# One load of a four-layer kernel's input, issued from ScalarE's queue in place of SyncE's

## The chip, the cores and the metric

The kernel runs on one core of a Trainium2 chip. The core has five engines with an instruction queue each: TensorE (PE, matrix products), VectorE (DVE), ScalarE (ACT), GpSimd (POOL) and SyncE (SP), which here does nothing but issue DMAs and wait. Loads and stores are carried by 16 DMA engines. The metric is the device time of one execution in microseconds; less is better. The profile comes from one further execution that the hardware profiler recorded.

## What is computed

Two blocks, run twice in turn on x of 2048 tokens by 512 features, in bfloat16. Each block normalises its input and adds its result to it.

```python
x = A_x
x = x + _A_ref(_layernorm(x, axis=-1), A_wqkv, A_wo)   # linear attention, 32 heads of 16
x = x + _B_ref(_layernorm(x, axis=-1), B_w1, B_w2)     # 512 -> 1376, relu, -> 512
x = x + _A_ref(_layernorm(x, axis=-1), A_wqkv, A_wo)
x = x + _B_ref(_layernorm(x, axis=-1), B_w1, B_w2)
```

In the attention block q, k and v are projections of the normalised x by `A_wqkv`; phi (t + 1 for positive t, exp(t) otherwise) is applied to q and k; k and v are summed over all tokens into one small matrix for each head, by which q is multiplied.

## The kernel before

The 2048 tokens are 16 tiles of 128 tokens, in four chunks of four tiles. x lies in `xin` with one tile in each of 16 slots. All operations of the four layers are put into a graph by `build_kernel`: each operation has an engine, what it reads and writes, and a cost. A planner (`_list_schedule`) then lays out each engine's order from these costs, from a table of hand-set priorities (`HINTS`) and a few fixed sequences (`SEQS`), and `emit_engine` writes one instruction stream for each engine, with semaphore waits where an operation needs another engine's result. Every DMA is an operation of SyncE, made by the helper `dma`, with a semaphore of its own that reaches 16 when the data has landed.

The start of the first layer is what the change and the prediction's steps touch. SyncE issues, in this order:

- tile 0 of x (`ld_x0_0`, line 744, 128 KB)
- tiles 1 to 3 of x (`ld_x0_1`, line 744, 384 KB)
- the k and q columns of `A_wqkv`, in two halves of the contraction (`ld_wqk0` and `ld_wqk1`, line 750, 512 KB each)
- tiles 4 and 5 (`ld_x1_0`, line 744, 256 KB)
- tiles 6 and 7 (`ld_x1_2`), which wait until tiles 1 to 3 have landed
- chunks 3 and 2 (512 KB each), behind the landing of the second and of the first half of the weights

```python
ld_x(0, 0, 1, 100.0)
wq_v = A_wqkv.rearrange("(c p) n -> p c n", p=128)
ld_x(0, 1, lat=1500.0)
```

Nothing before these loads is waited for but the barrier at the program's start.

Meanwhile TensorE runs warm-up matmuls on a constant (line 775), ScalarE waits for GpSimd's constant `nhalf` (line 783), loads its table of functions (line 763) and runs one small operation, and GpSimd sets up constants.

Chunk 0 is handled tile by tile. VectorE takes a tile's statistics (lines 802 and 803) and subtracts the mean (line 1554); for tile 3, ScalarE sums the tile and its squares instead (lines 1564 and 1566). TensorE transposes the centred tile (line 883), ScalarE or VectorE copies it from the accumulator memory into `Tb` (lines 887 and 888), and TensorE multiplies it by the weights (line 928, the helper that emits nearly all matrix products). GpSimd computes the reciprocal standard deviations (lines 1548 and 1550), which ScalarE applies when it reads the products (lines 910 and 912). VectorE's order begins with the statistics of tile 0, then those of tile 2, then the centring of tiles 2 and 3, and the statistics of tile 1. The products of k come in two halves, so that the first half of the weights can be used before the second has landed. From chunk 1 on, VectorE normalises whole tiles (lines 809, 845) and a DMA transpose that SyncE issues (line 866) fills `Tb`; the first of these waits for all weight loads.

## Time and profile before

| what | value |
|---|---|
| median of 3 runs | 267.29 us (267.24 to 267.83) |
| profiled execution, its own time | 267.75 us |
| span of the profile, first to last instruction | 266.0 us, 5120 instructions |
| TensorE busy | 260.9 us (98%) |
| VectorE, ScalarE, GpSimd busy | 215.4, 192.0, 51.2 us (81%, 72%, 19%) |
| DMA | 23.22 MB in 48122 packets, mean 87 GB/s |

Times in the profile are microseconds from the span's start. In a row of the timeline stand the start, the length, the engine, the line, the operation, what it writes and reads, the count, and in brackets the idle time of the engine just before with what ended it. "SPq" is SyncE's queue at a DMA issue; the transfer itself shows only as a wait of those who need the data ("DMA xin<-in_A_x_dram"). In a row of the windows stand the stretch, its length, the busy time (and count) of PE, PE's weight loads, DVE, ACT and POOL, the granted clock of TensorE, the busy share of the DMA engines, which can exceed 1 where transfers overlap, and GB/s. In a row of the DMA issues the last number is the time from issue to landing. The ends of matrix products are modelled, so a busy TensorE isn't one at its peak.

### The profile page before, as it was taken

The page shows a single profiled execution, that of the slowest core. Times are in us where ns is not written, and L with a number is a line of the kernel's source. Part 1 is how long each engine was busy: PE and PEld are TensorE (multiplying, and loading weights), DVE is VectorE, ACT ScalarE, POOL GpSimd, SP SyncE. Part 2 cuts the span into 40 slices and gives each one's busy share as a digit, 9 for nine tenths or more (in the row PEclk, how much of TensorE's full clock was granted, in tenths as well). Part 3 has the DMA queues.
Part 4 walks back from the last instruction along what each step waited for, and adds up shares of the span by engine and source line. Part 5 has one row for each costly group of instructions (what it writes and reads, how often), then busy time and mean ns, then how long its engine had stood idle before and what let it go on. Part 6 is the DMA issues. An engine that isn't in the chain of part 4 may idle for free.

```text
span 266.0 us, 5120 instructions
## 1 busy us (share of the span) xinstructions
PE 260.9 (98%) x1890; PEld 171.2 (64%) x1890; DVE 215.4 (81%) x557; ACT 192.0 (72%) x420; POOL 51.2 (19%) x131
## 2 busy tenths in 40 slices
PE   7999999999999999999999999999999999999996
PEld 3344444644755888767776744474488888888874
DVE  4897986799889999879786848479999888697865
ACT  4798899998975756898718689578599974656300
POOL 6410010012860023400001340001734040000000
PEclk9999999999999999999999999999999999999999
DMA  6744489866249023150000313054460501602104
GB/s 213 252 88 81 139 159 366 229 156 100 44 87 160 0 21 58 25 99 1 2 0 0 66 27 68 4 140 111 107 120 2 99 2 38 140 2 70 52 1 160
DMA packets 48122, 23.22 MB, mean 87 GB/s; under 512 B 38784, under 2 KB 45920, under 8 KB 48096
## 3 DMA queue, kind: packets, MB, share of 16 engines
q1 hardware_dynamic: 48096, 22.88, 37.2%
q8 instruction: 15, 0.25, 0.4%
q14 instruction: 11, 0.09, 0.1%
HBM read 7.14 MB, written 2.10 MB: 35 GB/s over the span
## 4 chain that ended last, share of the span: by engine, by line
PE 91%; DMA 4%; DVE 3%; SPq 1%; issue 0%; DVEq 0%
PE ps L928 91%; DMA xin<-in_A_x_dram 3%; DMA Tb<-xn 1%; DVE bst L802 1%; DVE big L921 1%; DVE xn L845 0%; DVE wqkv L944 0%; SPq L750 0%; SPq L744 0%; DVE escr L914 0%; DVE xn L1610 0%; DVE mv L803 0%; DVE veps L809 0%; DVEq L1822 0%
## 5 line engine op out<-in xcount | busy, mean ns | idle before, releaser
L928 PE MATMUL ps<-Tb,w 128*128 128x256 f16 (+2 forms) x240 | 42.0, 301 | 0.0
L1327 ACT ACTIVATE big<-ps 128x512 bf16<-128x512 f32 x58 | 33.0, 597 | 10.3 <-PE ps L928 10.0
L960 ACT ACTIVATE sqscr<-xres 128x512 bf16<-128x512 f32 x48 | 29.9, 626 | 9.6 <-DVE xres L954 9.4
L928 PE MATMUL ps<-w,big 128*128 128x256 bf16 (+5 forms) x213 | 36.5, 293 | 0.0
L928 PE MATMUL ps<-wqkv,Tb 128*128 128x512 bf16 x144 | 34.5, 379 | 0.9 <-DMA wqkv<-in_A_wqkv_dram 0.6
L928 PE MATMUL ps<-big,xn 128*128 128x512 bf16 (+1 forms) x160 | 31.2, 336 | 0.2 <-DVE veps L809 0.2
L910 ACT ACTIVATE big<-ps 128x512 bf16<-128x512 f32 x48 | 28.7, 603 | 1.5 <-PE ps L928 1.4
L928 PEld LDWEIGHTS ps<-Tb,w 128*128 128x128 f16 (+1 forms) x240 | 23.2, 98 | 9.3
L928 PE MATMUL ps<-xn,xin 128*128 128x256 f16 x168 | 28.8, 272 | 0.0
L1274 DVE TENSOR_TENSOR ps<-ps,escr 128x256 f32<-128x256 f32 x56 | 22.8, 427 | 7.1 <-PE ps L928 6.6
L912 ACT ACTIVATE escr<-ps 128x512 bf16<-128x512 f32 x44 | 25.7, 604 | 3.4 <-PE ps L928 3.3
L928 PE MATMUL ps<-Tb,wqkv 128*128 128x512 bf16 x112 | 27.1, 379 | 0.0
L825 POOL TENSOR_SCALAR mean<-s 128x4 f32<-128x4 f32 (+1 forms) x13 | 3.7, 285 | 117.4 <-DVE xres L954 117.3
L928 PE MATMUL ps<-Mf,big 128*128 128x512 bf16 x112 | 25.0, 379 | 0.0
L928 PEld LDWEIGHTS ps<-wqkv,Tb 128*128 128x128 bf16 x144 | 13.7, 98 | 16.5 <-DMA wqkv<-in_A_wqkv_dram 1.1
L928 PEld LDWEIGHTS ps<-w,big 128*128 128x128 bf16 (+1 forms) x213 | 20.3, 98 | 5.2
L928 PEld LDWEIGHTS ps<-big,xn 128*128 128x128 bf16 x160 | 15.1, 98 | 12.1 <-POOL xn L979 0.7
L928 PE MATMUL ps<-xin,big 128*128 128x256 bf16 x150 | 20.8, 272 | 0.0
L914 DVE TENSOR_SCALAR escr<-escr 128x512 bf16<-128x512 bf16 x52 | 14.3, 286 | 6.7 <-ACT escr L912 6.5
L928 PEld LDWEIGHTS ps<-Mf,big 128*128 128x128 bf16 x112 | 10.7, 98 | 12.7 <-DVE big L1105 0.3
L921 DVE TENSOR_TENSOR big<-big,escr 128x512 bf16<-128x512 bf16 x46 | 18.4, 417 | 0.2
L928 PEld LDWEIGHTS ps<-Tb,wqkv 128*128 128x128 bf16 x112 | 10.8, 98 | 11.7 <-issue 0.4
(139 smaller groups left out, 499.4 us busy)
## 6 DMA issues: line engine op xcount, KB each, us to landing
big<-rdc SPq DMA_DIRECT2D x32, 128.0 KB, 2.7
wqkv<-in_A_wqkv_dram SPq DMA_DIRECT2D x3, 512.0 KB, 5.0
w<-in_B_w_dram SPq DMA_DIRECT2D x1, 1376.0 KB, 7.6
w<-in_B_w_dram SPq DMA_DIRECT2D x1, 1280.0 KB, 10.8
xin<-in_A_x_dram SPq DMA_DIRECT2D x2, 512.0 KB, 4.5
out_dram<-wqkv SPq DMA_DIRECT2D x2, 512.0 KB, 3.5
xin<-in_A_x_dram SPq DMA_DIRECT2D x2, 256.0 KB, 6.2
wo<-in_A_wo_dram SPq DMA_DIRECT2D x1, 512.0 KB, 7.6
```

Source lines behind the costliest of these rows:

```text
L802: g.add(DVE, lambda e: e.bn_stats(bst[:, i, :], xin[:, i, :]), [("xin", i)] + list(after), [("bst", i)], C_DVE_BNST, name="bnst%d" % i)
L825: g.add(POOL, lambda e: e.tensor_scalar(mean[:, sl], s1[:, sl], -INV_D, None, ALU.mult), [("s1", i) for i in tl], [("mean", i) for i in tl ...
L910: g.add(ACT, lambda e: e.activation(dst_ap, psv[:, b, :], ACTF.Identity, bias=1.0 + 1e-6, scale=sc), [("ps", b)] + rk, [dst_key], C_ACT_PS ...
L912: g.add(ACT, lambda e: e.activation(esc, psv[:, b, :], ACTF.Exp, scale=sc), [("ps", b)] + rk, [ekey], C_ACT_EXP + xd, name=name + "_exp")
L914: g.add(DVE, lambda e: e.tensor_scalar(esc, esc, 1.0, 1e-6, ALU.min, ALU.add), [ekey], [ekey], C_DVE_BF4X, name=name + "_em")
L921: g.add(DVE, lambda e: e.tensor_tensor(dst_ap, dst_ap, esc, ALU.max), [dst_key, ekey], [dst_key], 340.0, name=name + "_phi")
L928: last = e.matmul(o, l, r, start=st, stop=sp, skip_group_check=skip)
L960: g.add(ACT, lambda e: e.activation(sqscr[:, q, :], xres[:, i, :], ACTF.Square, accum_out=s2[:, i:i + 1]), [("xres", i)], [("sqscr", q), ( ...
L1274: g.add(DVE, lambda e: e.tensor_tensor(psv[:, bank, 256:512], psv[:, Y, 0:256], m5, ALU.add), [("ps", Y), ("escr", s)], [("ps", bank)], C_ ...
L1327: g.add_flex([(ACT, lambda e: e.activation(unit_ap(u), psv[:, b, :], ACTF.Relu), C_ACT_PSUM), (DVE, lambda e: e.tensor_scalar(unit_ap(u), ...
```

## The change

The load of tiles 1 to 3 (`ld_x0_1`) is taken out of SyncE's stream and emitted as the first instruction of ScalarE's, with the same semaphore. The planner still sees the operation where it was, on SyncE and at the same cost, so every engine's order stays as it was; SyncE simply emits nothing at that place. The load waits for nothing, before or after. Those who wait for tiles 1 to 3 wait for the same semaphore.

```diff
+        ACT_LOADS = ('ld_x0_1',)
+        act_loads = []
...
             def _emit(eng, emit=emit, sem=sem):
                 return emit(eng).then_inc(sem, 16)
+            if g.layer == 0 and name in ACT_LOADS:
+                act_loads.append((ACT_LOADS.index(name), _emit))
+                _emit = lambda eng: None
             op = g.add(SP, _emit, reads, writes, dur=issue, lat=xfer_ns, dma=True, name=name)
...
             @block.scalar
             def _(s):
+                for _, load in sorted(act_loads, key=lambda a: a[0]):
+                    load(s)
                 emit_engine(ACT, s)
```

## The prediction

> **What bounds the kernel now.** I read the chain that ended last first, by line and then in order of time.

> ```profile
> by line: PE ps L928 91.1%; DMA xin<-in_A_x_dram 2.6%; DMA Tb<-xn 1.4%; DVE bst L802 0.9%; DVE big L921 0.5%; DVE xn L845 0.5%; DVE wqkv L944 0.4%; SPq L750 0.3%; SPq L744 0.3%; DVE escr L914 0.3%; DVE xn L1610 0.2%; issue 0.2%; DVE mv L803
> 0.79 0.40 SPq L744
> ...
> 1.25 0.41 SPq L744
> ...
> 1.71 0.43 SPq L750
> ...
> 2.18 0.47 SPq L750
> ...
> 2.69 6.87 DMA xin<-in_A_x_dram
> ...
> 9.58 1.29 DVE bst L802 x2
> ...
> 16.75 3.86 DMA Tb<-xn
> 20.61 0.05 issue
> 20.65 242.27 PE ps L928 x1790
> ```

> From 20.65 us on TensorE is the chain for 242 us, so the change is worth there what it moves the start of that stretch. Ahead of it lie five DMA issues, one after the other on SyncE. The second (1.25) is the load that moves; the fifth (2.69) is the first half of x's second chunk (tiles 4 and 5), which lands 6.87 us later and starts the statistics on VectorE at 9.58. From there to 16.75 the chain is VectorE's, and then a DMA transpose. Next, each engine in order of time:

> ```profile
> 2.88 0.69 DVE L802 BATCH_NORM_STATS2 bst<-xin 128x6 f32<-128x512 bf16 x1 [2.88 <-DMA xin<-in_A_x_dram]
> 3.83 0.35 DVE L1554 TENSOR_SCALAR xn<-xin,mv 128x512 bf16<-128x512 bf16 x1
> 4.66 0.70 DVE L802 BATCH_NORM_STATS2 bst<-xin 128x6 f32<-128x512 bf16 x1 [0.47 <-DMA xin<-in_A_x_dram]
> 7.99 0.42 DVE L888 COPY Tb<-ps 128x512 bf16<-128x512 bf16 x1
> 9.58 1.29 DVE L802 BATCH_NORM_STATS2 bst<-xin 128x6 f32<-128x512 bf16 x2 [1.18 <-DMA xin<-in_A_x_dram]
> 0.83 3.78 PE L775 MATMUL ps<-const-bfloat16-1.0 128*128 128x512 bf16 x9 [0.83 <-PEq L1877]
> 6.01 0.40 PE L883 MATMUL ps<-ident,xn 128*128 128x128 bf16 x4 [0.63 <-DVE xn L1554]
> 6.58 1.13 PE L928 MATMUL ps<-wqkv,Tb 128*128 128x512 bf16 x4
> 7.77 0.59 PE L928 MATMUL ps<-wqkv,Tb 128*128 128x512 bf16 x2
> 8.96 5.79 PE L928 MATMUL ps<-wqkv,Tb 128*128 128x512 bf16 x26 [0.60 <-DMA wqkv<-in_A_wqkv_dram]
> 14.95 3.19 PE L928 MATMUL ps<-big,xn 128*128 128x512 bf16 x16 [0.20 <-DVE veps L809]
> 20.65 0.60 PE L928 MATMUL ps<-wqkv,Tb 128*128 128x512 bf16 x2 [0.35 <-DMA Tb<-xn]
> ```

> The bracket is the idle time before a group and what ended it. VectorE waits 0.47 us for tiles 1 to 3 (the moved load, landed by 4.66). TensorE waits 0.63 for a centred tile, 0.60 for the second half of the projection weights (landed by 8.96), then 0.20 and 0.35: 1.78 us of waiting after its warm-up, the most that any earlier loading can remove. Last, what the DMA engines do in half-microseconds; the last two numbers are their busy share and GB/s:

> ```profile
> 2.00:2.50 0.50, 0.50 (x3) 0.16 (x2) 0.00 (x0) 0.00 (x0) 0.50 (x3) 1.00 1.26 260
> 2.50:3.00 0.50, 0.50 (x3) 0.22 (x2) 0.12 (x1) 0.38 (x1) 0.10 (x2) 1.00 0.77 190
> 4.00:4.50 0.50, 0.50 (x3) 0.20 (x2) 0.18 (x1) 0.12 (x1) 0.50 (x3) 1.00 0.54 172
> 7.50:8.00 0.50, 0.50 (x7) 0.36 (x6) 0.50 (x3) 0.31 (x1) 0.50 (x3) 1.00 1.00 389
> 8.50:9.00 0.50, 0.04 (x1) 0.04 (x2) 0.00 (x0) 0.00 (x0) 0.22 (x1) 1.00 0.17 66
> 9.00:9.50 0.50, 0.50 (x3) 0.26 (x4) 0.00 (x0) 0.00 (x0) 0.00 (x0) 1.00 0.06 25
> ```

> The first loads run as one stream, with dips to 190 and 172 GB/s early and 389 when it is full. From 9.00 to 9.50 only 25 GB/s move, a sixteenth of 389: one of the 16 engines is behind the others, and the pieces that TensorE and VectorE wait for at 8.96 and 9.58 are its own. That this engine is late in every execution I can't see; the runs of before lie at 267.24, 267.29 and 267.83, the profiled one at 267.75, which looks like two kinds, half a microsecond apart.

> **The change, part by part.** *SyncE loses one issue.* From 1.25 to 1.71 is 0.46 us. The three issues behind it (both weight halves, tiles 4 and 5) come 0.46 earlier. The next two pieces of the queue wait for landings:

> ```profile
> 4.65 0.34 SPq L744 DMA_DIRECT2D xin<-in_A_x_dram  x1
> 8.93 0.81 SPq L744 DMA_DIRECT2D xin<-in_A_x_dram  x2
> ```

> The first follows the landing of tiles 1 to 3, the other two that of the second weight half; they go where these go. GpSimd issues no loads here and nothing is moved past it.

> *ScalarE gains one issue.* Its price there no row shows. SyncE's rows give 0.40 to 0.47, from which it may lie far off on either side, from next to nothing to a microsecond. I take 0.45. ScalarE's first own instruction is covered:

> ```profile
> 2.62 1.28 ACT L763 ACT_TABLE_LOAD   x1 [2.62 <-POOL nhalf L783]
> 4.66 0.63 ACT L1564 ACTIVATE sqscr<-xin 128x512 bf16<-128x512 bf16 x1 [0.54 <-DMA xin<-in_A_x_dram]
> ```

> It waits for GpSimd until 2.62, and behind the table load there is 0.54 more. An issue from about 0.8 has 1.8 us of cover, so I charge nothing; were it over 2.3 us, the excess would delay the mean of tile 3 and with it the wait of 0.63 on TensorE. No wait is added: the load had none.

> *The load itself starts 0.46 earlier* (0.79 in place of 1.25), beside tile 0 and not behind it. In the window of the first 12 us:

> ```profile
> xin<-in_A_x_dram SPq DMA_DIRECT2D x1, 384.0 KB, 3.4
> xin<-in_A_x_dram SPq DMA_DIRECT2D x1, 128.0 KB, 2.1
> ```

> With the same 3.4 us it lands at 0.79 + 3.4 = 4.19 in place of 4.66. Tile 0 now shares the engines with it. Bounds for its delay: nothing, if its pieces go first; 0.50, if both get equal shares (another 128 KB at the 260 GB/s of 2.00 to 2.50); 1.5, if all 384 KB go first. I take 0.25, between the first two, since both are issued at the same moment and tile 0 is the smaller. VectorE's part on tile 0 ends at 3.83 + 0.35 = 4.18, now 4.43, and the next statistics start there in place of 4.66: the chain of chunk 0 gains 0.23.

> *The weights and tiles 4 and 5.* If the stream is only moved, they land 0.46 earlier: TensorE's wait at 8.96 ends at 8.50, VectorE's at 9.12. Both engines are free by then (TensorE at 7.77 + 0.59 = 8.36, VectorE at 7.99 + 0.42 = 8.41). The later stalls of 0.20 and 0.35 hang on VectorE's work after 9.58 and move with it. Bounds: nothing gained, if the engines' rate and not the issue sets the landing; a gain beyond 0.46, if the starts overlap: the dip at 2.50 costs 0.5 x (1 - 190/389) = 0.26 us, that at 4.00 costs 0.28. Both gone as well would make 1.00. I take 0.46, the row it is nearest to. [...] The trace bears out the one stream (389 GB/s, flat, when full), but shows no second issuer.

> **The sum.** Against the profiled execution: 267.75 - 0.46 = 267.29 (its span is 266.0, with 1.75 around it that I leave alone). The median of the runs is 267.29, 0.46 below the profiled one. If its typical execution lacks the late DMA engine, the weights and tiles 4 and 5 are there up to 1 us sooner, neither wait at 8.96 and 9.58 exists, and the chain of chunk 0 decides, which gains 0.23. Between 0.23 and 0.46 I take the middle: 267.29 - 0.35 = **266.94 us**, faster by 0.13%. About 0.2% (0.53 us) is what a measurement of this kernel can tell from no change, so this is a forecast of no difference that can be told.

> **The rivals.**

> *The starts overlap (faster).* With two queues the engines have tiles 1 to 3 to move while tile 0's reads begin, and the first weights while tiles 1 to 3 run; the dips at 2.50 and 4.00 fill. Gain between 0.46 + 0.26 = 0.72 and 1.00, cut by TensorE: the chunk's own chain lets it go on at 8.36 at the earliest, a gain of 0.60, to which the later 0.35 adds at most. For it: the dips stand at the starts of loads. Against it: in a typical execution the chain of chunk 0 would cap it. About -0.65: 266.6.

> *Nothing moves.* The issues of the two engines are made one at a time, so the second load still begins after 1.2 us and the weights no sooner; or the load isn't late but the engines' rate is the limit. Within 0.15 of the median: 267.3. For it: five issues of 0.40 to 0.47 in a row on SyncE never overlap. Against it: they are one engine's. [...]

> *Tile 0 is pushed back (slower).* Everything on VectorE, TensorE and ScalarE begins with tile 0, landed by 2.88. If the engines take tiles 1 to 3 turn by turn with it or ahead of it, tile 0 comes 0.5 to 1.5 us later. VectorE has 0.47 of idle time behind tile 0; a delay of more than 0.47 is the point from which chunk 0 is later than before, and every microsecond beyond it moves the projections at 6.58. A delay of 1.0 costs 0.53; in the profiled execution TensorE's wait of 0.60 would cover that, in a typical one nothing does. There is a second price in the same place: the nine warm-up matmuls (eight of 512 columns, one of 256) take 3.78 us, 0.87 ns a column, the later ones about half (5.79 / 26 = 0.22 us for 512 columns, 0.43 ns a column), so TensorE is at half rate at the start; were it to stay so for longer because it idles after 4.61, six projection matmuls would cost 6 x 0.22 = 1.3 more. About +0.55: 267.85. [...] No run of before has two queues of loads, so the trace can't say.

> That the change doesn't do what it says I leave out: the emitted load is the same call with the same semaphore, at the head of the other queue.

> **How the numbers follow.** Forecast (266.8 to 267.15) 0.40; starts overlap 0.25; nothing moves 0.12; tile 0 pushed back 0.23. Faster by over 0.2% means under 266.76: nearly all of the second case and 0.05 of the first, 0.28. Slower means over 267.82: most of the last, up to a delay with the half-rate price, 0.18. The rest is 0.54. The range leaves out a tenth on each side: low 266.4, about the sum of a gain of 0.60 and the later 0.35 at its most; high 267.9, a delay of tile 0 of 1.1 us.

> **What would show it.** Right: in the chain the issues on SyncE run 0.79, 1.25 (weights), 1.71, and tiles 4 and 5 at 2.2; the table load stays at 2.62; VectorE's second statistics start between 4.2 and 4.5 without a wait, its statistics of tiles 4 and 5 near 9.1; TensorE's wait for weights ends near 8.5, and the stretch of 242 us starts near 20.2. Overlap: GB/s above 250 from 2.00 on, the wait at 8.96 gone. Pushed back: VectorE's first statistics after 3.35, and TensorE's first transpose after 4.9. It would be wrong as a whole if the space around the span (1.75 us) grew because a second engine's queue is in use; no row of before can show that.

## The result, and the profile after

The changed kernel is slower: 268.60 us median of 22 runs (267.25 to 269.66) against 267.51 for the kernel before (22 runs, 266.94 to 268.44), a ratio of 1.0035 with a 95% interval of 1.0021 to 1.0050. The runs fall into two groups: 10 lie from 267.25 to 267.83, about where the kernel before lies, and 12 from 268.53 to 269.66; between 267.83 and 268.53 there is none. The profiled execution, 269.52, is one of the upper group.

First the chain of the changed kernel, in order of time. Its line numbers are 5 higher than before: L933 is what L928 was, L807 what L802 was.

```profile
0.79 3.42 DMA xin<-in_A_x_dram
4.21 0.02 issue
4.23 0.71 DVE bst L807
...
5.59 0.40 PE ps L888 x2
...
8.05 1.71 PE ps L933 x4
9.75 0.44 PE ps L888 x4
10.19 0.02 issue
10.22 0.42 DVE Tb L893
10.64 1.19 DVE bst L807 x2
...
17.84 4.04 DMA Tb<-xn
21.88 0.05 issue
21.93 242.27 PE ps L933 x1790
```

The chain no longer begins with SyncE's issues and the load of tiles 4 and 5. It begins with tile 0, which lands 3.42 us after its issue, and runs through chunk 0: its statistics, the transposes, four projection matmuls in 1.71 us. TensorE's long stretch is as long as before, 242.27 us, and starts at 21.93 in place of 20.65. So 1.28 us are lost, all of them ahead of 22 us. Of the 1.8 us by which the span grew (266.0 to 267.8) the rest, 0.5 us, lies behind the chain's last operation, where the last stores take longer to land (1.9 us for the very last, 1.5 before).

Now the same start by engine, from the timeline of the changed kernel:

```profile
0.78 0.40 ACTq L749 DMA_DIRECT2D xin<-in_A_x_dram  x1
0.79 0.40 SPq L749 DMA_DIRECT2D xin<-in_A_x_dram  x1
1.25 0.95 SPq L755 DMA_DIRECT2D wqkv<-in_A_wqkv_dram  x2
2.24 6.60 SPq L749 DMA_DIRECT2D xin<-in_A_x_dram  x4
2.62 1.28 ACT L768 ACT_TABLE_LOAD   x1 [2.62 <-POOL nhalf L788]
4.04 0.63 ACT L1569 ACTIVATE sqscr<-xin 128x512 bf16<-128x512 bf16 x1
4.23 0.69 DVE L807 BATCH_NORM_STATS2 bst<-xin 128x6 f32<-128x512 bf16 x1 [4.23 <-DMA xin<-in_A_x_dram]
5.45 0.69 DVE L807 BATCH_NORM_STATS2 bst<-xin 128x6 f32<-128x512 bf16 x1
5.59 0.40 PE L888 MATMUL ps<-ident,xn 128*128 128x128 bf16 x2 [0.98 <-DVE xn L1559]
6.42 0.42 PE L780 MATMUL ps<-const-bfloat16-1.0 128*128 128x256 bf16 x1
7.84 1.91 PE L933 MATMUL ps<-wqkv,Tb 128*128 128x512 bf16 x4
10.56 1.27 DVE L807 BATCH_NORM_STATS2 bst<-xin 128x6 f32<-128x512 bf16 x2
```

What was meant to move, moved: the two loads are issued at 0.78 and 0.79, the weights at 1.25, tiles 4 and 5 at 2.24, and the table load is where it was. ScalarE reads tile 3 at 4.04, so tiles 1 to 3 are there by then. Tile 0 isn't: VectorE starts on it at 4.23, later than ScalarE on tile 3, and 1.35 us later than before (2.88). TensorE then idles for 0.98 us before the first transposes, and its matmuls afterwards take longer than they did: one of 256 columns 0.42 us (0.27 before), the group of four projections 1.91 (1.13 before). In the chain the four take 1.71 us, 0.83 ns a column, which is about the 0.87 of the warm-up and twice the 0.43 of the later matmuls: the half rate. The wait for weights is gone, and so is VectorE's for tiles 4 and 5, which it reaches only at 10.56 (9.58 before). The same small matmul in the kernel before:

```profile
5.11 0.27 PE L775 MATMUL ps<-const-bfloat16-1.0 128*128 128x256 bf16 x1
```

The DMA issues of the first 12 us of the changed kernel, the last number being us to landing:

```profile
xin<-in_A_x_dram ACTq DMA_DIRECT2D x1, 384.0 KB, 3.2
xin<-in_A_x_dram SPq DMA_DIRECT2D x1, 128.0 KB, 3.4
```

Three times the bytes landed in less time. Before, tile 0's load, alone at the head of the queue, took 2.1 us and the other 3.4. The view of the DMA queues from 2.50 to 3.00 us (packets, MB, share) has ScalarE's queue as q10 and SyncE's as q1, which at that time carries tile 0:

```profile
q10 hardware_dynamic: 46, 0.14, 73.0%
q1 hardware_dynamic: 45, 0.05, 25.9%
```

In this stretch the two queues move nearly one packet for one (46 and 45), but a packet of tiles 1 to 3 is three times as large as one of tile 0 (0.14 and 0.05 MB). Over the whole load the 384 KB are 144 packets, and e2, which swaps the queues, counts 144 for the 128 KB. So here the engines took the two loads by turns of about a packet, and the small load landed 0.2 us behind the large one (3.4 and 3.2 us after issues 0.01 apart). Equal turns weren't equal bytes.

The DMA engines' windows in the changed kernel (share and GB/s at the end):

```profile
2.00:2.50 0.50, 0.50 (x3) 0.16 (x2) 0.00 (x0) 0.00 (x0) 0.50 (x3) 1.00 0.69 217
2.50:3.00 0.50, 0.50 (x3) 0.22 (x2) 0.00 (x0) 0.38 (x1) 0.10 (x2) 1.00 0.99 375
4.00:4.50 0.50, 0.50 (x2) 0.00 (x0) 0.27 (x1) 0.50 (x2) 0.00 (x0) 1.00 1.07 418
5.00:5.50 0.50, 0.00 (x0) 0.00 (x0) 0.46 (x3) 0.00 (x0) 0.27 (x1) 1.00 0.81 217
```

The stretches from 2.50 (190 before) and 4.00 (172) are filled, but there is a dip from 5.00 (352 before). The later loads come sooner all the same: tiles 4 and 5 land 6.4 us after their issue at 2.24, at about 8.6 (9.56 before). The one that everything waits for comes later. The column before the share, the granted clock, says 1.00 here too; in this profile the half rate shows in the matmuls' lengths alone.

### The profile page after: what moved, and what is told of

Read it like the earlier page. It is cut to its first block, busy times and chain, and to the rows that moved or that the text cites. A ratio compares the mean times of both kernels' runs of the same rounds, so it can differ in the third digit from the quotient of the medians.

```text
span 267.8 us, 5120 instructions
## 1 busy us (share of the span) xinstructions
PE 262.5 (98%) x1890; PEld 172.4 (64%) x1890; DVE 215.5 (80%) x557; ACT 191.9 (72%) x420; POOL 50.9 (19%) x131
## 4 chain that ended last, share of the span: by engine, by line
PE 92%; DVE 4%; DMA 3%; issue 0%; DVEq 0%
PE ps L933 91%; DMA Tb<-xn 2%; DMA xin<-in_A_x_dram 1%; DVE bst L807 1%; PE ps L888 1%; DVE big L926 1%; DVE xn L850 0%; DVE wqkv L949 0%; DVE escr L919 0%; PE ps L780 0%; DVE mv L808 0%; DVE xn L1615 0%; DVE Tb L893 0%; DVE xn L1559 0%; DVE veps L814 0%
## 5 line engine op out<-in xcount | busy, mean ns | idle before, releaser
L933 PE MATMUL ps<-Tb,w 128*128 128x256 f16 (+2 forms) x240 | 42.0, 301 | 0.0
L933 PE MATMUL ps<-w,big 128*128 128x256 bf16 (+5 forms) x213 | 36.5, 293 | 0.0
L933 PE MATMUL ps<-wqkv,Tb 128*128 128x512 bf16 x144 | 35.1, 387 | 0.5 <-DMA Tb<-xn 0.5
L933 PE MATMUL ps<-big,xn 128*128 128x512 bf16 (+1 forms) x160 | 31.2, 336 | 0.0
L933 PEld LDWEIGHTS ps<-Tb,w 128*128 128x128 f16 (+1 forms) x240 | 23.1, 98 | 9.3
L933 PE MATMUL ps<-xn,xin 128*128 128x256 f16 x168 | 28.8, 272 | 0.0
L933 PE MATMUL ps<-Tb,wqkv 128*128 128x512 bf16 x112 | 27.1, 379 | 0.0
L933 PE MATMUL ps<-Mf,big 128*128 128x512 bf16 x112 | 25.0, 379 | 0.0
L933 PEld LDWEIGHTS ps<-wqkv,Tb 128*128 128x128 bf16 x144 | 14.2, 100 | 15.9 <-DMA Tb<-xn 0.8
L933 PEld LDWEIGHTS ps<-w,big 128*128 128x128 bf16 (+1 forms) x213 | 20.3, 98 | 5.2
L933 PEld LDWEIGHTS ps<-big,xn 128*128 128x128 bf16 x160 | 15.2, 98 | 11.7 <-issue 0.7
L933 PE MATMUL ps<-xin,big 128*128 128x256 bf16 x150 | 20.8, 272 | 0.0
L933 PEld LDWEIGHTS ps<-Mf,big 128*128 128x128 bf16 x112 | 10.7, 98 | 12.7 <-DVE big L1110 0.3
L933 PEld LDWEIGHTS ps<-Tb,wqkv 128*128 128x128 bf16 x112 | 10.8, 98 | 11.7 <-issue 0.4
## 6 DMA issues: line engine op xcount, KB each, us to landing
big<-rdc SPq DMA_DIRECT2D x32, 128.0 KB, 2.7
```

The lines of the kernel that those rows point to most:

```text
L933: last = e.matmul(o, l, r, start=st, stop=sp, skip_group_check=skip)
```

## The experiments

The theory after this reading had two prices. **One:** tile 0 is pushed back, because the DMA engines take up both loads at once. **Two:** TensorE stays at half rate for some microseconds more in the executions of the upper group, because it idles before its first work. The rivals: the second queue costs something by itself; only the late tile counts. Ratios are each to the kernel before on the same chip; the last three columns are of the one profiled execution of each.

| kernel | median us (range, runs) | ratio (95%) | first statistics at | four projections take | TensorE's stretch starts |
|---|---|---|---|---|---|
| before | 267.51 (266.94 to 268.44, 22) | | 2.88 | 1.13 | 20.65 |
| changed | 268.60 (267.25 to 269.66, 22) | 1.0035 (1.0021 to 1.0050) | 4.23 | 1.91 | 21.93 |
| e1, tile 0 first | 266.86 (266.37 to 267.56, 12) | 0.9969 (0.9957 to 0.9981) | 2.98 | 1.08 | 19.46 |
| e2, queues swapped | 267.55 (267.13 to 269.45, 12) | 1.0017 (0.9997 to 1.0037) | 3.96 | 1.13 | 20.18 |
| e3, three more warm-ups | 268.46 (268.09 to 268.71, 9) | 1.0034 (1.0021 to 1.0046) | 4.43 | 1.13 | 20.65 |
| e4, one queue, swapped | 269.24 (267.88 to 270.10, 8) | 1.0060 (1.0040 to 1.0080) | 4.28 | 1.55 | 21.23 |
| e5, longer warm-up | 267.47 (267.29 to 267.80, 11) | 1.0010 (1.0001 to 1.0019) | 4.32 | 1.12 | 20.36 |
| e6, short warm-up | 268.18 (267.95 to 268.55, 6) | 1.0030 (1.0018 to 1.0042) | 2.87 | 1.91 | 21.46 |
| e7, changed again | 268.91 (267.60 to 269.40, 6) | 1.0056 (1.0038 to 1.0075) | 4.31 | 1.57 | 21.27 |
| e8, two more warm-ups | 267.64 (267.19 to 268.05, 11) | 1.0014 (1.0006 to 1.0023) | 4.31 | 1.13 | 20.53 |

The kernel before ran at 267.57 beside e1 to e4 and at 267.25 beside e5 to e8.

### e1: tile 0 gets a lead

```diff
             def _(s):
+                s.wait_ge(sem_eng[POOL], 1)
                 for _, load in sorted(act_loads, key=lambda a: a[0]):
```

> The changed kernel, but ScalarE waits for GpSimd's first operation (done near 1.0 us) before it issues the load of tiles 1 to 3. Theory (tile 0 is pushed back because both loads are taken up at once): tile 0 has a lead again, VectorE's first statistics start before 3.1 us in place of 4.23, the transposes begin before 4.7, and the time is at or under that of before, 266.9 to 267.6. Rival (a load from a second queue costs by itself, wherever it stands): the statistics still start late or the time stays near 268.6.

Timeline of e1:

```profile
1.02 0.38 ACTq L749 DMA_DIRECT2D xin<-in_A_x_dram  x1
2.98 0.69 DVE L807 BATCH_NORM_STATS2 bst<-xin 128x6 f32<-128x512 bf16 x1 [2.98 <-DMA xin<-in_A_x_dram]
4.20 0.69 DVE L807 BATCH_NORM_STATS2 bst<-xin 128x6 f32<-128x512 bf16 x1
8.27 1.27 DVE L807 BATCH_NORM_STATS2 bst<-xin 128x6 f32<-128x512 bf16 x2
5.94 0.42 PE L780 MATMUL ps<-const-bfloat16-1.0 128*128 128x256 bf16 x1
```

and from its chain:

```profile
15.54 3.88 DMA Tb<-xn
19.46 5.35 PE ps L933 x24
```

A lead of 0.23 us (issued at 1.02, not 0.79) is enough: tile 0 is at 2.98, nearly as early as before, the tiles behind it are taken at 4.20 without a wait, tiles 4 and 5 at 8.27 without a wait (9.58 before). The long stretch starts 1.19 us sooner than before. The load still comes from ScalarE's queue, so the rival that this queue costs by itself falls. TensorE goes from its warm-up to the transposes without idling, and all 12 runs lie in one group up to 267.56. (It is at half rate at 5.94 even so, and at full rate for the four projections.) The time is a little under what was expected. This version beats both kernels, by 0.31% (0.19 to 0.43%) against the one before.

### e2: the queues swapped

```diff
-        ACT_LOADS = ('ld_x0_1',)
+        ACT_LOADS = ('ld_x0_0',)
```

> The queues are swapped: tile 0 from ScalarE, tiles 1 to 3 from SyncE, both at about 0.8 us. If the engines share between the two loads by turns, tile 0 is as late as in the changed kernel (statistics from 3.9 to 4.4) and the time is 268.2 to 269. If ScalarE's queue is simply taken up a little sooner and what is taken up first goes first, tile 0 lands by 3.1, tiles 1 to 3 by about 4.6, and the time is at or under that of before, 266.9 to 267.6.

From e2's DMA issues in the first 12 us:

```profile
xin<-in_A_x_dram SPq DMA_DIRECT2D x1, 384.0 KB, 3.4
xin<-in_A_x_dram ACTq DMA_DIRECT2D x1, 128.0 KB, 3.2
```

Tile 0 is late from the other queue too (3.96 in place of 2.88), and lands about when the load three times its size does. So the engines shared between the two here too (3.2 us for the 128 KB, 3.4 for the 384); neither queue was simply served first. The time was not as expected: 267.55, no difference that can be told. The runs show why: 7 lie from 267.13 to 267.58 and 5 from 268.43 to 269.45, two groups as in the changed kernel, with another share in each. The profiled execution, 267.29, is one of the lower group, and its matmuls are short:

```profile
5.32 0.28 PE L888 MATMUL ps<-ident,xn 128*128 128x128 bf16 x2 [0.71 <-DVE xn L1559]
5.77 0.27 PE L780 MATMUL ps<-const-bfloat16-1.0 128*128 128x256 bf16 x1
```

A late tile 0 without the half rate, then, lies near the time of before.

### e4: one queue, tiles 1 to 3 first

All loads on SyncE, as in the kernel before; tile 0's issue is held back behind that of tiles 1 to 3.

```diff
+            if g.layer == 0 and name == "ld_x0_0":
+                held.append(_emit)
+                _emit = lambda eng: None
+            elif g.layer == 0 and name == "ld_x0_1":
+                _emit = lambda eng, own=_emit: (own(eng), held[0](eng))
```

> The kernel before, with all loads on SyncE, but tiles 1 to 3 issued ahead of tile 0. Theory (the order of the bytes is what costs, not the queue): tile 0 lands at 3.9 to 4.4 us and the time is like that of the changed kernel, 268 to 269.5. Rival (the second queue costs): tile 0 lands no later than 3.5, and the time stays under 267.8.

From e4's timeline (its lines are again 1 higher):

```profile
4.28 0.69 DVE L808 BATCH_NORM_STATS2 bst<-xin 128x6 f32<-128x512 bf16 x1 [4.28 <-DMA xin<-in_A_x_dram]
5.64 0.40 PE L889 MATMUL ps<-ident,xn 128*128 128x128 bf16 x2 [1.03 <-DVE xn L1560]
6.47 0.42 PE L781 MATMUL ps<-const-bfloat16-1.0 128*128 128x256 bf16 x1
```

As the theory has it: without any second queue, a tile 0 that lands behind 384 KB brings the same lateness, the same idle TensorE and the same half rate, and costs 0.60% (0.40 to 0.80%). That this is more than the change costs (0.35%, and 0.56% in e7) isn't shown: the intervals overlap.

### e3: three more warm-up matmuls, a miss

```diff
-                    for n in cols:
+                    for n in (cols + [512] * 3 if name == "warm" else cols):
```

> The changed kernel with three more warm-up matmuls of 512 columns, which fill TensorE's idle time of 0.98 us ahead of the first transposes; nothing waits for them but TensorE's own order. Theory (two prices: tile 0 late, and TensorE longer at half rate because it idled): the runs of 268.5 to 269.7 vanish and all lie at 267.3 to 267.9; tile 0 stays at 4.2, and matmuls of 256 columns after 5.6 us take 0.27 us and not 0.42. Rival (only the late tile counts): the time stays near 268.6, with runs up to 269.7.

TensorE's idle time ahead of the transposes shrank to 0.55 us. The runs near 269 are gone (highest 268.71), but the rest isn't at 267.5; all 9 lie around 268.46. The half rate is gone too: four projections in 1.13 us, the stretch starting at 20.65 as before. The loss lies elsewhere, in one row of TensorE's timeline, far behind the start:

```profile
68.07 2.13 PE L933 MATMUL ps<-Tb,w 128*128 128x256 bf16 x15 [0.71 <-DMA Tb<-xn]
```

TensorE waits 0.71 us for a DMA transpose; none of the other profiles shows a wait there. In the DMA view of 56 to 70 us the transposes of e3 take 5.5 us to land,

```profile
Tb<-xn SPq DMA_TRANSPOSE x2, 5.5
```

and those of e2 3.6:

```profile
Tb<-xn SPq DMA_TRANSPOSE x2, 3.6
```

And e3 fetches instructions in the midst of them, as its view of the DMA queues from 64 to 66 us shows (packets, MB, share):

```profile
q8 instruction: 1, 0.02, 2.9%
```

In the same stretch of e2, whose long stretch starts 0.47 us earlier, there is no packet of that queue; its fetch comes between 67.5 and 69.5. The kernel before, with its transposes issued at 62.22 as in e3, has none there either, and they take 3.6. e1 does have one between 64 and 66, and its transposes take 4.3 us, without a wait on TensorE. Three matmuls more may have moved TensorE's instructions along, and the fetch may have delayed the transpose; both are the author's estimate from the two standing together, not shown. e5 and e8 test what matters here, whether a longer warm-up costs in itself.

### e5 and e8: warm-up to the same end with fewer instructions more

e5 keeps eight warm-up matmuls and makes the last one longer (the profile shows this one as two instructions, so one more than in the changed kernel), e8 adds two in place of three. The diff is e5's; e8's is e3's line with 2 in place of 3.

```diff
+                        if k == 7:
+                            last = e.matmul(psv[:, wt, 0:384], one_wf, one_mf[:, 0:384], start=True, stop=True)
+                            continue
```

> The changed kernel, with the last of the eight warm-up matmuls of 512 columns replaced by one of 384 columns in float32, which should keep TensorE busy until about 5.4 us with no more instructions than before. Three more warm-ups had given 268.46, and its profile shows TensorE waiting 0.71 us for a DMA transpose near 67 us, beside a code fetch of the instruction queue, which the changed kernel doesn't show. Theory (half rate after an idle TensorE is the second price, and the wait near 67 us came from moving the instructions): no runs of 268.5 to 269.7, all at 267.2 to 267.9, no wait near 67 us, and matmuls of 256 columns at 0.27 us after 5.6. Rival (a longer warm-up costs in itself, or half rate isn't the price): 268.3 or more.

> The changed kernel with two more warm-up matmuls of 512 columns in place of three. It keeps TensorE busy until about 5.4 us. Theory: no runs of 268.5 to 269.7 from half rate. If the wait near 67 us hangs on where the instructions stand, it may go or stay with four instructions more in place of six: 267.2 to 267.9 without it, 268.1 to 268.6 with it, and a code fetch beside it in the trace only in the second case. Rival (a longer warm-up costs in itself): 268.3 with no such wait.

From e5's timeline:

```profile
3.76 1.49 PE L783 MATMUL ps<-const-float32-1.0 128*128 128x384 f32 x2
5.67 0.39 PE L893 MATMUL ps<-ident,xn 128*128 128x128 bf16 x2 [0.21 <-DVE xn L1564]
7.12 0.27 PE L785 MATMUL ps<-const-bfloat16-1.0 128*128 128x256 bf16 x1
```

The idle time before the transposes is 0.21 us in place of 0.98 (0.20 in e8). All 11 runs of e5 lie from 267.29 to 267.80 and all 11 of e8 from 267.19 to 268.05: the upper group is gone, though tile 0 is as late as ever (4.32 and 4.31). Neither profile has the wait near 67 us. So the upper group is the half rate's, and the long half rate comes with the idle TensorE; e1, with the shorter warm-up but no idle time, has no upper group either. In detail e5 missed: its profile still has 0.39 us for 256 columns at 6.50, and 0.27 only from 7.12; the projections, from 7.45, are at full rate, which is what counts.

The idle time doesn't decide alone. In the profiles with about 1 us of it (changed 0.98, e4 1.03, e7 1.06) the half rate reaches into the projections, past 8 us; in e2, after 0.71 us, TensorE is at full rate by 5.77, and in e1, with none, it is still at half rate at 5.94. What sets the moment isn't shown.

### e6: the half rate alone

The kernel before, with tile 0 as early as ever, and the warm-up cut short.

```diff
-                    for n in cols:
+                    for n in ([128] * 8 if name == "warm" else cols):
```

> The kernel before, all loads on SyncE, with the eight warm-up matmuls of 512 columns cut to 128 columns each, so that TensorE idles from about 2 us until tile 0 is centred near 4.2. Tile 0 is as early as before. Theory (half rate is a price of its own, paid when TensorE idles before the chunk's work): matmuls of 256 columns take 0.42 us until past 7, and the time is 268.2 to 269.4. Rival (only the late tile counts): within 0.3 of the kernel before.

From e6's timeline:

```profile
2.87 0.69 DVE L802 BATCH_NORM_STATS2 bst<-xin 128x6 f32<-128x512 bf16 x1 [2.87 <-DMA xin<-in_A_x_dram]
4.23 0.39 PE L883 MATMUL ps<-ident,xn 128*128 128x128 bf16 x2 [2.18 <-DVE xn L1554]
6.90 1.91 PE L928 MATMUL ps<-wqkv,Tb 128*128 128x512 bf16 x4
```

268.18 against 267.25: the half rate, with nothing late, costs 0.30% (0.18 to 0.42%), just under what was expected. The four projections take 1.91 us as in the changed kernel. The rival that only the late tile counts falls.

### e7: the changed kernel again

Unaltered.

> The changed kernel once more, unaltered, for a second profile beside the others of this call. Theory: two groups of runs, near 267.5 and near 269.1; tile 0's statistics start at 3.9 to 4.5 in any case, and whether matmuls of 256 columns after 5.6 us take 0.27 or 0.42 us tells which group the profiled execution is in. Rival (one group, spread by the DMA engines): the time doesn't go with the matmuls' length.

One run at 267.60, five from 268.46 to 269.40. The profiled execution, 268.46, has its first statistics at 4.31 and its projections at half rate for part of the time:

```profile
5.67 0.40 PE L888 MATMUL ps<-ident,xn 128*128 128x128 bf16 x2 [1.06 <-DVE xn L1559]
7.92 1.57 PE L933 MATMUL ps<-wqkv,Tb 128*128 128x512 bf16 x4
```

It stands between: 1.57 us for the four, and a time at the lower edge of the upper group, where the profile of 269.52 has 1.91. In these two profiles the time goes with the matmuls' length; the changed kernel has no profile of a run of the lower group, for which e2's, e5's and e8's stand.

## Why the prediction was wrong, point by point

- **SyncE's issues** 0.46 sooner: right (weights at 1.25, tiles 4 and 5 at 2.24). **ScalarE's issue** at no price: right, 0.40 us at 0.78, the table load still at 2.62. **Tiles 1 to 3** at 4.19: a little sooner, ScalarE reads them at 4.04. **The rival that nothing moves** fell: the two issues stand at 0.78 and 0.79 and take 0.40 us each, as one alone does.
- **Tile 0's delay**, "I take 0.25, between the first two, since both are issued at the same moment and tile 0 is the smaller": this is the step that failed. It was 1.35 us (4.23 against 2.88), and 1.08 to 1.55 in the profiles of e2, e3, e5, e7 and e8, about the upper bound of 1.5 that was the price of all 384 KB going first. The 0.25 lay below the bound of equal shares (0.50), which are shares in bytes; the queues took nearly equal turns by packets (45 and 46 in the half-microsecond from 2.50), 144 for each load, and so the two landed together. In place of a gain of 0.23, chunk 0 had a loss of 0.79 (VectorE's second statistics at 5.45, not 4.66), and the idle TensorE brought the half rate, which the sum had at nothing.
- **The weights and tiles 4 and 5**, 0.46 sooner: the sign was right, the size too small. In e1, where nothing hides it, VectorE takes tiles 4 and 5 at 8.27 without a wait, 1.31 before its time in the profile of before. Part of this is that they were late in that profile: in e6, which has the loads of the kernel before, they land at 8.9 (issued at 2.69, 6.2 us), in e1 at 8.1 (issued at 2.21, 5.9 us). That is 0.8 sooner, of which 0.48 is the issue. The rival that the starts overlap had this in part: the stretches at 2.50 and 4.00 are filled, though the changed kernel shows a dip at 5.00. Its price of about 0.65 us is close to what e1 gained (267.57 to 266.86, 0.71). A gain of one issue slot, 0.46, is what the prediction took here; what e1 measured lies above it (0.71, by the interval of the ratio 0.51 to 1.15).
- **The rival "tile 0 is pushed back"** had the mechanism, the place and both prices, and was given 0.23. Its sum of +0.55 took a delay of 1.0 and left the half rate out; with the half rate the changed kernel lies 1.1 above the median of before. How the engines divide two queues no run of before could show; in these runs 128 KB and 384 KB, 144 packets each, landed within 0.2 us of each other from either queue (3.4 and 3.2 us after issue, 3.2 and 3.4 in e2).
- **The half rate** was priced at up to 1.3 us and thought an aside. It is the larger part of the verdict: with it removed (e5, e8) the change costs 0.10 and 0.14%, with it 0.35 and, on the chip of e5 and e8, 0.56% (e7). The medians of the two groups of the changed kernel, 267.52 and 269.22, are 1.7 us apart; in e6 the half rate costs 0.9. Why it costs less there is open. When the full rate comes is open too: behind the same 3.8 us of warm-up it came by 5.11 in the profile of before, after 5.94 in e1, and after 8 us where TensorE had idled for about 1 us (0.98 to 1.06). What sets the moment no run shows.
- **The late DMA engine** of the profiled execution, and with it the reading of the runs of before as two kinds: not tested. That it isn't late in every execution e6 shows, where tiles 4 and 5 land at 8.9 in place of 9.56.

## What to carry to other kernels

In these runs a second queue made two loads share the DMA engines (tile 0 at 4.23 in place of 2.88); put there only what may wait, and give the load that everything waits for a lead, here 0.23 us through a semaphore that is there anyway (tile 0 at 2.98 in e1). A first-needed piece was not protected by being small: count packets (144 for 128 KB as for 384), not bytes. Where a warm-up is cut to end just as the first data arrive, a later arrival can be paid twice, as in the changed kernel's profile, once as a wait (0.98 us on TensorE) and once as matmuls at half rate (0.42 us for 256 columns, not 0.27); look at the matmuls' length right behind the idle time.
